# Plain float32 for the first block of a fused attention and feed-forward kernel

## The chip, the cores and the metric

The kernel runs on one core of a Trainium2 chip. The metric is the time of one execution on the device in microseconds; the median over several runs counts.

## The reference

A linear attention without softmax, a norm by head, and a feed-forward block with softplus. q, k, v have the shape 8 x 8 x 576 x 64 (batch, heads, sequence, head dimension), the two weight matrices are 512 x 2048 and 2048 x 512 and come in float64, as words of eight bytes.

```
kv  = einsum('bhsd,bhse->bhde', k, v)
out = einsum('bhsd,bhde->bhse', q, kv)
rms = sqrt(mean(out * out, axis=-1, keepdims=True) + 1e-06)
x   = (out / rms * g_norm).transpose(0, 2, 1, 3).reshape(4608, 512)
h   = x @ w_in
g   = maximum(h, 0) + log1p(exp(-abs(h)))
y   = g @ w_out                                  # 4608 x 512
```

## The kernel before

**Divided operands.** Large multiplications run in the format float32r, in which a multiplication rounds its operands. To keep float32 accuracy each operand is divided into a high part, a low part times 4096 and a third part that mends the product of both, and each product is three float32r multiplications into the same bank. Dividing an operand takes an operation on ScalarE (ACT) and two on VectorE (DVE): `high`, `low`, `less`. A weight's parts come from `split_weight`; for the eight weights of the first four chunks the third part is a sum made by two matmuls with the identity and its negative (`less_by_pe`, L525 and L526).

**Weights.** Weight number j belongs to chunk c = j // 2 of 128 hidden units; even j is a piece of w_in, odd j a piece of w_out. `weight` fetches it as two words for each value (512 KB) and makes a float32 of it: a square on ACT (L434), six operations on DVE (L438, L442, L447, L455, L460, L464), and an operation on ACT that counts values out of range (L451). There is one buffer `raw`, another `rawb`, and one `sq`. g of the norm is multiplied in when a piece of w_in is divided (L501, L508).

**Attention.** `kv_of(b)` loads k and v of a batch in four main parts and a tail and multiplies them (L696). `rows(t)` makes tile t of 128 tokens: q is turned (L776 on TensorE (PE) for the first two batches), multiplied by kv (L720), squared on ACT (L793), reduced on DVE (L724), its root taken on GpSimd (POOL, L727 and L728), scaled on DVE (L732), and turned (L738). The first six tiles are divided from the bank (`split`, L640, L643, L646) and stored to memory for later as well (L802, L803).

**Feed-forward.** The first stage walks over 12 blocks of 384 tokens, and in each over the first four or six chunks: `step(s)` is the multiplication by w_in (`mm1`, L864, 12 matmuls of 384 columns), softplus (L886), the division of g (L888, L875, L879) and the multiplication by w_out (`mm2`, L871, nine matmuls of 512 columns). Steps 0 to 3 are block 0, step 4 opens block 1. Two later phases do the other chunks in wide steps of 512 tokens with a scheme that saves multiplications (L1066, L1137), 48 of them.

**The order of the work.** Each operation is a task with an engine, an estimated duration, what it waits for, the buffers it takes and frees, and a position. `Plan.order` writes the order for every engine from these: an engine takes, of what can start first by the estimates, the task with the lowest position. The lists P0 to P7 are such positions. Where PE would stand idle by the estimates for 400 ns before step 6, a dummy matmul is put in (`warm`, L1232). The engines then run their lists strictly in order, and all DMAs of note are issued by SyncE (SP).

Of the kernel before, what the change touches and what calls it, by code (L numbers as in the profile page):

```python
# [22 lines left out]
DOWN_G = 1.0 - 0.99 * 2.0 ** -13  # L23
E = 1.0 / RADIX

# [181 lines left out]
def kernel(  # L207
# [47 lines left out]
    P0 = [-45.94, -26.77, -11.8, 0.28, -29.91, -5.64, -2.86, 3.84, -103.4, -98.98, -69.3, -76.66, -68.5, -24.67, -23.22, -34.97, 8.15, -43.02, 7.47, 9.69, 7.18, 18.16, -12.1, 4.75, 1.0, 106.19, 31.3, 6.28, 7.19, 5.22]  # L255
    P4 = [-30.17, -6.08, 16.93, -33.9, -22.35, -28.91, -17.33, -7.12, -18.68, -2.69, 0.62, 2.73, -7.38, -1.86, 1.1, 1.72, 5.22, -13.65, 3.22, 0.88, 43.88, 43.95, -0.17, -0.32, 44.8, 40.82, -20.17, -6.56, 6.41, 10.03, -10.73, 0.23, 2.8, 0.42, -9.48, -5.03]
    P5 = [1.24, -5.69, -2.28, -3.57, 1.72, 0.53, 6.68, -5.83, 3.01, -2.95, 3.35, 1.4, -6.96, 0.27, -5.34, -2.29]
    P6 = [1.05, 6.24, 4.29, 4.08, -1.52, -2.85, 1.21, -0.34, 3.11, 3.1, -1.07, -0.73, -0.88, 9.99, 5.7, 5.69, 0.13, 0.46]
    P7 = [-23.78, -17.98, -11.85, -14.93, 0.41, 1.61, 7.35, 2.7, -25.02, -6.6, -15.2, -4.48, -2.14, 0.64, 2.93, 0.97, 4.67, 5.36, 3.33, 6.57, -10.37, 2.36, -14.11, -9.89, -7.11, 12.91, -2.89, 14.55, 12.59, 9.35]
    CONVERT, FETCH, EARLY, LATER = P0[:8], P0[8:16], P0[16:27], P0[27:]  # L260
    P1 = [49.11, 48.77, 51.0, 80.9, 122.61, 131.29, 2.87, 53.84, 71.21, 480.08, 304.47, 150.69]
    P2 = [24.08, 35.56, 23.68, 37.26, 50.08, 83.13, 74.26, 112.0, 102.25, 108.09, 139.38, -110.13, 88.34, 208.35, 423.47, -209.77, 170.15, -245.78, 423.49, 179.94, -7.53]
    P3 = [2.14, 2.48, 6.41, -16.53, 0.86, 2.79, 4.01, -16.44, 3.79, 3.96, 2.19, 1.79, 0.72, 1.35, 1.55, -1.03]
# [3 lines left out]
    EARLIER = P3[15]  # L267
    PACE = 2.5
    BY_PE = 12
    AT_ONCE = 2 * TB  # L270

# [10 lines left out]
    g_down = const.tile([P, 1], F32, name="g_down")  # L282
# [24 lines left out]
    pieces = sb.tile([P, 12, PIECE], F32R, name="pieces")  # L307
    for i in range(3):
# [4 lines left out]
    minus_r = space("gv1", 4 * WIDE, False, F32R)[:, 3 * NT:3 * NT + P]  # L313
# [5 lines left out]
                 h=2, o=2, tp=1, s0=1, s1=1, s2=1, s3=1, w=15, wh=3, u=4, u1=1, gvp=2, xl=2, ab=2)  # L319
# [7 lines left out]
    heirs.update({("w", 12 + i): [("n", 3 * i + j) for j in range(3)] for i in range(3)})  # L327
    plan = Plan(rings, heirs)
    slot, add = plan.slot, plan.add

    def new(s, shape, dtype=F32):
# [17 lines left out]
        elif r == "w":  # L349
            s.tile = shaped(pieces[:, i] if i < 12 else space(f"w{i}", PIECE, True, F32R), shape, dtype)  # L350
        elif r == "n":
            s.tile = shaped(space(f"w{12 + i // 3}", PIECE, False)[:, i % 3 * d_model:], shape, dtype)
        elif r == "wh":
# [46 lines left out]
    factors_done = {}  # L400
# [13 lines left out]
    def weight(j, pos, fetch_pos, behind):  # L414

        c, of_out = divmod(j, 2)
        raw, w = slot("rawb" if j % 2 and c < 8 else "raw"), slot("m")
# [9 lines left out]
        if wide:  # L427
# [30 lines left out]
            def rest():  # L458
                pf = p.tile.bitcast(F32)
                nc.vector.scalar_tensor_tensor(out=pf, in0=words_of()[0], scalar=2.0 ** -52, in1=pf,  # L460
                                               op0=ALU.mult, op1=ALU.mult)

            def total():
                nc.vector.tensor_tensor(out=new(w, [P, d_model]), in0=t.tile.bitcast(F32),  # L464
                                        in1=p.tile.bitcast(F32), op=ALU.add)
# [6 lines left out]
            d4 = add("DVE", 430, power, [d3], pos, [p, w])  # L472
# [5 lines left out]
        if c < OWN:  # L478
            divide(j, w, ready, pos, c < 4)
# [11 lines left out]
    def split_weight(w, part_of, n, dst, ready, pos, of_in, by_pe=False):  # L491
# [21 lines left out]
        def low_up():  # L513
            nc.scalar.activation(dst.tile[:, 1], d.tile, func=AF.Copy, scale=RADIX)
# [753 lines left out]
```

## Time and profile before

| | |
|---|---|
| median of 3 runs | 857.7 us (857.61 to 859.12) |
| profiled execution, first to last instruction | 856.4 us |
| PE busy | 843.0 us, 98% |
| DVE busy | 704.1 us, 82% |
| ACT busy | 520.6 us, 61% |
| POOL busy | 76.6 us, 9% |
| moved by DMA | 167.07 MB, 195 GB/s over the span |

The span covers the instructions of the profiled execution; the difference to the median lies around them. Busy time of PE counts the dummy matmuls too, and ends of matmuls are modelled, so PE's share says little about the first microseconds.

### The profile page before, as it was taken

To read this page: it belongs to the slowest core of one execution; us is meant where nothing else is said; L and a number is where in the kernel's file an instruction comes from. 1 tells how busy PE (TensorE), PEld (TensorE's weight loads), DVE (VectorE), ACT (ScalarE), POOL (GpSimd) and SP (SyncE) were. 2 spreads that over 40 slices of the span, in tenths; PEclk is the share of its full clock that TensorE was granted. 3 is DMA by queue.
4 is the path that set the end of the run, shared out by engine and by line. 5 is a ranking of instruction groups with operands and counts; after the bars stand their busy time and mean duration, and the time that the engine had idled before them with its cause. 6 is when DMAs were issued, how large, how long until landed. Compare 5 with 4: busy or idle time off the path is not lost.

```text
span 856.4 us, 17075 instructions
## 1 busy us (share of the span) xinstructions
PE 843.0 (98%) x6464; PEld 754.1 (88%) x6464; DVE 704.1 (82%) x995; ACT 520.6 (61%) x980; POOL 76.6 (9%) x79
## 2 busy tenths in 40 slices
PE   8899999999999999999999999999999999999998
PEld 5578898999898999999999999998999899999996
DVE  7888898888788889798898788878788766788873
ACT  6766665446344567766667665655868555566654
POOL 0351223111113300000000000000000000000000
PEclk9999999999999999999999999999999999999999
DMA  9998997778884755436644546645364753777864
GB/s 283 297 233 212 261 273 232 185 245 218 214 188 119 194 160 185 142 110 207 210 156 154 180 151 206 195 158 181 124 197 138 234 168 102 240 237 246 249 189 131
DMA packets 239778, 167.07 MB, mean 195 GB/s; under 512 B 106320, under 2 KB 198736, under 8 KB 239696
## 3 DMA queue, kind: packets, MB, share of 16 engines
q1 hardware_dynamic: 239392, 165.86, 65.9%
q8 instruction: 50, 0.82, 0.4%
q14 instruction: 32, 0.26, 0.1%
q10 hardware_dynamic: 304, 0.13, 0.1%
HBM read 112.98 MB, written 52.95 MB: 194 GB/s over the span
## 4 chain that ended last, share of the span: by engine, by line
PE 94%; ACT 1%; DVE 1%; DMA 1%; issue 1%; POOL 0%; SPq 0%; POOLq 0%; DVEq 0%; ACTq 0%
PE banks L1137 31%; PE banks L1066 28%; PE banks L871 16%; PE banks L864 15%; PE banks L720 2%; PE banks L696 2%; DMA loads<-in_k_dram 1%; PE banks L738 0%; PE banks L1232 0%; PE banks L776 0%; DVE units L643 0%; DVE half L732 0%; DVE roots L724 0%; POOL roots L728 0%; ACT w L783 0%
## 5 line engine op out<-in xcount | busy, mean ns | idle before, releaser
L1137 PE MATMUL banks<-pieces,gv 128*128 128x512 f32 x768 | 236.8, 390 | 0.0
L1137 PE MATMUL banks<-pieces,g_False 128*128 128x512 f32 x384 | 149.4, 389 | 0.0
L1137 PEld LDWEIGHTS banks<-pieces,gv 128*128 128x128 f32 x768 | 132.5, 188 | 17.2 <-DVE banks L910 0.2
L864 PE MATMUL banks<-units,pieces 128*128 128x384 f32 x768 | 144.8, 337 | 0.0
L871 PE MATMUL banks<-pieces,gv 128*128 128x512 f32 x576 | 143.3, 393 | 0.0
L864 PEld LDWEIGHTS banks<-units,pieces 128*128 128x128 f32 x768 | 134.7, 188 | 4.5
L871 PEld LDWEIGHTS banks<-pieces,gv 128*128 128x128 f32 x576 | 106.2, 188 | 19.0
L1066 PEld LDWEIGHTS banks<-units,pieces 128*128 128x128 f32 x840 | 111.0, 188 | 6.5 <-ACT banks L1112 0.4
L1066 PE MATMUL banks<-units,pieces 128*128 128x256 f32 x840 | 115.2, 280 | 0.0
L886 ACT ACTIVATE half<-banks 128x384 f32<-128x384 f32 x64 | 31.4, 491 | 94.0 <-PE banks L864 90.7
L1127 DVE TENSOR_TENSOR gv<-g_True,gv 128x1024 fp32r<-128x1024 f32 x47 | 57.5, 1223 | 35.6 <-ACT gv L1124 35.5
L1137 PEld LDWEIGHTS banks<-pieces,g_False 128*128 128x128 f32 x384 | 72.1, 188 | 15.0
L1066 PEld LDWEIGHTS banks<-units,w 128*128 128x128 f32 x504 | 66.7, 188 | 3.7 <-ACT banks L1112 0.2
L1066 PE MATMUL banks<-units,w 128*128 128x256 f32 x504 | 69.6, 280 | 0.0
L728 POOL TENSOR_TENSOR roots<-roots,half 128x8 f32<-128x8 f32 x36 | 62.3, 1731 | 3.0
L1130 DVE SCALAR_TENSOR_TENSOR g_False<-gv 128x1024 fp32r<-128x1024 f32 x47 | 57.6, 1225 | 1.5
L1029 DVE TENSOR_TENSOR units<-loads,units 128x1024 fp32r<-128x1024 f32 x42 | 51.2, 1219 | 6.0 <-ACT units L1026 5.9
L1094 ACT ACTIVATE g_True<-banks 128x256 f32<-128x256 f32 x96 | 36.7, 384 | 30.6 <-PE banks L1066 29.9
L1116 DVE TENSOR_TENSOR g_True<-banks,g_True 128x512 f32<-128x512 f32 x48 | 33.1, 690 | 25.8 <-PE banks L1066 19.8
L931 ACT ACTIVATE m<-banks 128x512 f32<-128x512 f32 x72 | 42.1, 595 | 18.2 <-PE banks L1137 12.5
L1032 DVE SCALAR_TENSOR_TENSOR units<-units 128x1024 fp32r<-128x1024 f32 x42 | 51.4, 1224 | 1.7
L1026 ACT ACTIVATE units<-loads 128x1024 fp32r<-128x1024 f32 x42 | 44.3, 1056 | 12.4 <-PE banks L1066 10.1
(115 smaller groups left out, 1248.7 us busy)
## 6 DMA issues: line engine op xcount, KB each, us to landing
loads<-x SPq DMA_DIRECT2D x180, 128.0 KB, 2.7
part<-m SPq DMA_DIRECT2D x72, 256.0 KB, 3.1
m<-part SPq DMA_DIRECT2D x72, 256.0 KB, 3.4
loads<-form SPq DMA_DIRECT2D x45, 256.0 KB, 3.2
form<-loads SPq DMA_DIRECT2D x36, 256.0 KB, 3.0
raw<-in_moe_w_in_dram SPq DMA_DIRECT2D x16, 512.0 KB, 4.7
loads<-in_k_dram SPq DMA_DIRECT2D x32, 256.0 KB, 4.0
loads<-in_v_dram SPq DMA_DIRECT2D x32, 256.0 KB, 4.5
```

The lines of the kernel that those rows point to most:

```text
L728: nc.gpsimd.tensor_tensor(out=r.tile, in0=r.tile, in1=half, op=ALU.pow)
L864: nc.tensor.matmul(from_the_end(hp, w), lhsT=w_in.tile[:, i, kd * P:(kd + 1) * P], rhs=from_the_end(xv.tile[:, i, kd], w), start=(m == 0), ...
L871: nc.tensor.matmul(mine[i].tile, lhsT=gv.tile[:, m, i * P:(i + 1) * P], rhs=w_out.tile[:, m], start=(c == cs[0] and m == 0), stop=(c == cs ...
L931: a = add("ACT", 690 if ph == LAST else 600, lambda: nc.scalar.activation(new(ot, [P, d_model]), bank.tile, func=AF.Copy, scale=scale if p ...
L1026: nc.scalar.activation(part_of(0, F32R), xl.tile if m > 1 else xl.tile[:, 0], func=AF.Copy, scale=DOWN)
L1029: nc.vector.tensor_tensor(out=part_of(1, F32R), in0=xl.tile if m > 1 else xl.tile[:, 0], in1=part_of(0), op=ALU.subtract)
L1032: nc.vector.scalar_tensor_tensor(out=part_of(2, F32R), in0=part_of(1), scalar=-RADIX, in1=part_of(0), op0=ALU.mult, op1=ALU.add)
L1066: nc.tensor.matmul(from_the_end(place(q), (16, 8)[kd]), lhsT=w[:, m, at:at + P], rhs=from_the_end(dst.tile[:, m, v, kd] if u < 6 else dst. ...
L1094: nc.scalar.activation(dst, src, func=AF.Softplus, scale=1.0 + E)
L1127: nc.vector.tensor_tensor(out=gvt(1, F32R), in0=gt(), in1=gvt(0), op=ALU.subtract)
L1130: nc.vector.scalar_tensor_tensor(out=gt(F32R), in0=gvt(1), scalar=-RADIX, in1=gvt(0), op0=ALU.mult, op1=ALU.add)
L1137: nc.tensor.matmul(from_the_end(mine[i].tile, P), lhsT=(gvt(m, F32R) if m < 2 else gt(F32R))[:, c, i * P:(i + 1) * P], rhs=from_the_end(ou ...
```

## The change

Block 0 (`PLAIN = 1`) is multiplied in plain float32 with whole operands: `plain_step` does `mm1` with 4 matmuls of 384 columns and `mm2` with 3 of 512, and softplus goes straight into `mm2`. In steps 0 and 1 (`BY_TILES = 2`) `mm1` is done tile by tile, 12 matmuls of 128 columns, each tile as soon as it is there. x of block 0 is copied whole from the bank by ACT, and stored from that copy. The weights of chunks 0 to 3 are kept whole in a ring `f` of eight places; they are divided for block 1 at positions of their own (`DIVIDE`).

The pieces' buffers w1 to w11 hold other things while no piece needs them: two more buffers for raw weights (`rawc`, for chunks 1 and 3), four for the later parts of batch 0's k and v (`k0`), the eight whole weights, x of block 0 (`xf`).

g of the norm is multiplied in while a piece of w_in is made (`rest` and `total`). The division of a weight has two operations on ACT and two on DVE, with a scale that saves the third on ACT; the signs of `low` and `less` change with it, and the matmuls L525 and L526 fall away. All positions are new.

```diff
-    pieces = sb.tile([P, 12, PIECE], F32R, name="pieces")
+    pieces = sb.tile([P, 1, PIECE], F32R, name="pieces")
+    for i in range(1, 12):
+        space(f"w{i}", PIECE, False)
...
-        raw, w = slot("rawb" if j % 2 and c < 8 else "raw"), slot("m")
+        raw, w = slot("rawc" if c in (1, 3) else "rawb" if j % 2 and c < 8 else "raw"), slot("f" if c < 4 else "m")
...
+                    nc.vector.scalar_tensor_tensor(out=y, in0=tf, scalar=g_col, in1=pf, op0=ALU.mult, op1=ALU.add)
...
         if c < OWN:
-            divide(j, w, ready, pos, c < 4)
+            if c < 4:
+                plain[of_out, c] = w, [ready]
+                pos = DIVIDE[j]
+            divide(j, w, ready, pos, c < 4 and BANKED)
...
+            nc.scalar.activation(new(dst, [P, 3, n], F32R)[:, 0], src(), func=AF.Copy, scale=DOWN * E)
         def low():
+            nc.vector.scalar_tensor_tensor(out=dst.tile[:, 1], in0=dst.tile.bitcast(F32)[:, 0], scalar=RADIX, in1=src(),
+                                           op0=ALU.mult, op1=ALU.subtract)
-        def low_up():
-            nc.scalar.activation(dst.tile[:, 1], d.tile, func=AF.Copy, scale=RADIX)
+        def both_of():
+            f32 = dst.tile.bitcast(F32)
+            nc.vector.tensor_tensor(out=new(d, [P, n]), in0=f32[:, 0], in1=f32[:, 1], op=ALU.add)
...
-            ks, vs = (slot(f"tail{i}" if tail else "e") for i in range(2))
+            ks, vs = (slot(f"tail{i}" if tail else "k0" if not b and p > 1 else "e") for i in range(2))
...
+            def whole():
+                nc.scalar.copy(part_of_x(), x.tile)
+            def store():
+                nc.sync.dma_start(out=x_of(t), in_=part_of_x())
...
+    def plain_step(s, n, c, cs, h, g, xv, mine):
+        (w_in, in_done), (w_out, out_done) = plain[0, c], plain[1, c]
+        def mm1(i0=0, n=TB):
+            hp = (h.tile if i0 else new(h, [P, NT]))[:, i0 * P:(i0 + n) * P]
+            for kd in range(KD):
+                nc.tensor.matmul(hp, lhsT=w_in.tile[:, kd * P:(kd + 1) * P], rhs=xv.tile[:, kd, i0 * P:(i0 + n) * P],
+                                 start=(kd == 0), stop=(kd == KD - 1))
+        def mm2(i):
+            if c == cs[0]:
+                new(mine[i], [P, d_model])
+            nc.tensor.matmul(mine[i].tile, lhsT=g.tile[:, i * P:(i + 1) * P], rhs=w_out.tile,
+                             start=(c == cs[0]), stop=(c == cs[-1]))
...
+        if s < BY_TILES:
+            made = []
+            for i in range(TB):
+                made.append(add("PE", 910, lambda i=i: mm1(i, 1), [x_split[n][i]] + in_done + made[-1:], s + 0.1 * i,
+                                [] if i else [h], last, follows=None))
+            a = made[-1]
+        else:
+            a = add("PE", 2670, mm1, x_split[n] + in_done + [m for _, m in mm1s[-1:]] +
+                    (plain[1, ORDER[s - 2][1]][1] if s > 1 else []), s, [h], last)
...
+            a2 = add("PE", 880, lambda i=i: mm2(i), [a] + out_done + [mm2s.get(i)], s + AFTER,
+                     [mine[i]] if c == cs[0] else [], [g] + ([w_out] if n == PLAIN - 1 else []))
```

202 lines of the change are left out of this document (121 added, 81 removed).

## The prediction

> **What bounds the kernel now.** I read the page first, then the busy time by stage, then the instructions of TensorE by shape, then the timeline of the first 80 us.
>
> ```profile
> span 856.4 us, 17075 instructions
> PE 843.0 (98%) x6464; PEld 754.1 (88%) x6464; DVE 704.1 (82%) x995; ACT 520.6 (61%) x980; POOL 76.6 (9%) x79
> ```
> ```profile
> 0.00:44.09 44.09, 35.90 (x464) 25.97 (x465) 37.01 (x67) 31.51 (x61) 10.32 (x17) 1.00 1.01 285
> 44.09:78.84 34.75, 33.32 (x437) 27.55 (x436) 30.05 (x52) 22.32 (x45) 13.59 (x13) 1.00 0.89 226
> 78.84:357.38 278.54, 278.54 (x2417) 251.27 (x2416) 239.79 (x411) 154.94 (x305) 52.65 (x50) 1.00 0.73 200
> 357.38:852.60 495.22, 495.22 (x3153) 449.27 (x3151) 396.77 (x467) 311.39 (x570) 0.00 (x0) 1.00 0.58 182
> ```
> The columns of the second fence are the stage and its length, then busy time of PE, its weight loads, DVE, ACT, POOL, the granted clock, the DMA share and GB/s. From 78.84 us on PE is busy in every microsecond; a gain can only come from what lies before. There even the busy time flatters:
>
> ```profile
> L1232 PE MATMUL banks<-ident_r 128*128 128x512 f32 x52 | 18.8, 480 | 2.0 <-DVE ident_r L1192 1.6 <-ACT pieces L529 0.2
> L864 PE MATMUL banks<-units,pieces 128*128 128x384 f32 x60 | 11.7, 342 | 0.0
> L871 PE MATMUL banks<-pieces,gv 128*128 128x512 f32 x36 | 9.5, 399 | 0.0
> L696 PE MATMUL banks<-loads 128*64 128x64 f32 x224 | 8.9, 226 | 2.0 <-DMA loads<-in_v_dram 1.1 <-DMA loads<-in_k_dram 0.7 <-DVE units L643 0.2
> L720 PE MATMUL banks<-early,w 64*64 64x64 f32 x384 | 7.7, 223 | 1.2 <-ACT half L793 0.6 <-ACT w L802 0.4
> ```
> This is the window up to 78.84 us. L1232 is the dummy multiplication that fills gaps, 52 times. L864 stands 60 times: five first multiplications of twelve, so at 78.84 us step 5 begins. I compare the two kernels at that point, the start of step 5 (the second step of block 1), since PE is full from there on.
>
> **The price of plain float32.** Two rows of the chain give the dense rate of the divided steps:
>
> ```profile
> 123.58 4.20 PE banks L864 x24
> 127.78 4.08 PE banks L871 x18
> ```
> 4.20/24 = 0.175 us for 384 columns, 4.08/18 = 0.2267 us for 512: (0.2267 - 0.175)/128 = 0.404 ns a column, and 0.020 us fixed. A plain float32 multiplication that fills the array is not in the trace; L696 and L720 are plain float32 on parts of the array, 64 columns, with two records for each instruction of the program. Their record lasts 226 and 223 ns. The durations of L864 and L871 (342 and 399) rise by 0.445 ns a column from 171 ns, so 64 columns passed once would be 200 ns and passed twice 228 ns. So two passes for each of two records: four. A plain instruction then costs 4 x columns x 0.404 ns + 2 x 0.020 us: 0.867 us at 512, 0.660 at 384, 0.247 at 128. The new block 0 has 12, 8 and 24 of them: 10.4 + 5.3 + 5.9 = 21.6 us on PE. It drops 48 of L864 and 36 of L871: 8.4 + 8.2 = 16.6 us. PE gets 5.0 us more to do there; that all is bought for an earlier start.
>
> The Trainium skill, in "TensorE: Matmul & The Clock Gate", section Back-to-back issue gap, gives columns / 2.4 GHz + 2.5 ns for an isolated matmul: 162.5 ns at 384 and 215.8 at 512, less than the 175 and 226.7 that this trace has. By the page four passes each would come to an estimated 20.9 us, 0.7 us under my sum.
>
> **When the first multiplication can start.** Before, it waits for three divided tiles of x and the divided weights, at 44.09 us. In the changed program tile 0 alone does, against whole weights. What the list of its instructions shows ahead of that:
>
> ```profile
> 0.00:10.00 10.00, 7.48 (x39) 5.26 (x41) 6.57 (x16) 4.17 (x6) 1.06 (x7) 1.00 0.83 254
> 10.00:20.00 10.00, 8.52 (x93) 6.04 (x90) 8.84 (x16) 7.75 (x15) 0.00 (x0) 1.00 1.09 319
> raw<-in_moe_w_in_dram SPq DMA_DIRECT2D x16, 512.0 KB, 4.7
> loads<-in_k_dram SPq DMA_DIRECT2D x32, 256.0 KB, 4.0
> ```
> ```profile
> 4.73 0.43 DVE L438 TENSOR_SCALAR m<-raw 128x512 uint32<-128x512 uint32 x1 [1.68 <-DMA raw<-in_moe_w_in_dram]
> 18.62 0.69 PE L696 MATMUL banks<-loads 128*64 128x64 f32 x16 [0.72 <-DMA loads<-in_k_dram]
> 22.83 1.28 DVE L724 TENSOR_REDUCE roots<-half 128x8 f32<-128x512 f32 x2 [0.48 <-ACT half L793]
> 25.08 0.69 DVE L511 TENSOR_TENSOR m<-m,pieces 128x512 f32<-128x512 f32 x1
> 25.69 0.69 DVE L732 TENSOR_TENSOR half<-banks,roots 128x512 f32<-128x512 f32 x1
> 27.18 0.60 ACT L640 ACTIVATE units<-banks 128x512 fp32r<-128x512 f32 x1 [0.75 <-PE banks L738]
> ```
> DMA: before, the last main load of batch 0's k and v is the end of 4.98 MB in SP's list. With 2.54 MB by 10 us and 319 GB/s after, that is 17.65 us; its matmul starts at 18.62, so 1.0 us later. In the new list six weights stand ahead of that load instead of four, 6.29 MB in all: 10 + 3.75/0.319 + 1.0 = 22.8 us, 4.2 us later than before. From that matmul to the first reduce of a tile are 22.83 - 18.62 = 4.2 us: 27.0 us.
>
> DVE: a weight's conversion is L438, L442, L447, L455, L460 and L464, 0.42 + 0.69 + 0.69 + 0.42 + 0.69 + 0.69 = 3.6 us by these groups of the whole run:
>
> ```profile
> L438 DVE TENSOR_SCALAR m<-raw 128x512 uint32<-128x512 uint32 x24 | 10.0, 415 | 2.0 <-DMA raw<-in_moe_w_in_dram 1.9
> L442 DVE SCALAR_TENSOR_TENSOR m<-raw,m 128x512 uint32<-128x512 uint32 x24 | 16.6, 690 | 0.6
> L455 DVE TENSOR_SCALAR m<-m 128x512 uint32<-128x512 uint32 x32 | 13.6, 424 | 1.2 <-DMA part<-m 0.4
> L464 DVE TENSOR_TENSOR m<-m,m 128x512 f32<-128x512 f32 x32 | 22.0, 687 | 0.7
> L451 ACT ACTIVATE sq<-sq,big 128x512 bf16<-128x512 bf16 x32 | 23.0, 717 | 8.1 <-DVE m L447 7.8
> L451 ACT ACTIVATION_READ_ACCUMULATOR sq<-sq,big 128x1 f32 x32 | 6.1, 190 | 0.0
> ```
> (the two not shown have L442's shape). Ahead of the first reduce the new DVE list has three whole conversions, a fourth but for its last operation, two operations each of three more, and four operations of dividing: 10.8 + 2.9 + 3.3 + 2.8 = 19.8 us. From 4.73 us on, with 2.1 us idle until the third weight (3.93 MB, 15.4 us) lands, that is 26.6. DMA and DVE meet at 27.0.
>
> From the reduce to the tile in SBUF took 27.18 + 0.60 - 22.83 = 4.95 us, which gives 31.95. But ACT now has ahead of that copy the count of what lies out of range (0.72 us and its 0.19 read) for a weight whose mask is the eighth operation of DVE from the reduce on; that is done at 31.9, the count at 32.9, the copy at 33.5. So the first useful multiplication starts at 33.5 us, 10.6 us earlier. It is not 10.6 us of gain, as PE has by then done less: the new list has three groups of k and v and several turns and rows still to come.
>
> **From there to step 5.** PE's list between: 21.6 us of plain float32, one L864 step (2.1 us), 3.5 turns of q, 7 of x, 8 of rows, 8 groups of k and v. Their start-to-start times:
>
> ```profile
> 39.48 0.66 PE L776 MATMUL banks<-ident_r,w 128*128 128x128 f32 x4
> 40.07 0.69 PE L720 MATMUL banks<-early,w 64*64 64x64 f32 x32
> ...
> 51.86 1.15 PE L696 MATMUL banks<-loads 128*64 128x64 f32 x32 [0.21 <-DVE units L643]
> 52.95 0.69 PE L720 MATMUL banks<-early,w 64*64 64x64 f32 x32
> 53.57 2.38 PE L864 MATMUL banks<-units,pieces 128*128 128x384 f32 x12
> ...
> 78.43 0.66 PE L738 MATMUL banks<-ident_r,half 128*128 128x128 f32 x4
> 78.84 2.36 PE L864 MATMUL banks<-units,pieces 128*128 128x384 f32 x12
> ```
> A turn of q 0.59, two groups of k and v 1.09, rows 0.62, a turn of x 0.41: 2.1 + 4.4 + 5.0 + 2.9. With the 23.7 above it is 38.0 us. I add 1.0 us for tile 2, whose copy comes eight ACT operations behind its norm. Step 5 at 33.5 + 38.0 + 1.0 = 72.5 us, if nothing else waits.
>
> What can wait is W_out of chunk 1: its total stands last in DVE's list, 40 operations after the first reduce, and the second multiplication of step 1 needs it. PE reaches that one at 33.5 + 19.1 + 1.0 = 53.6. The 40 are 35 of 0.69 and 5 of 0.42. Independent neighbours start 0.61 us apart (L511 to L732 above), dependent ones 0.72: with 0.65, 22.8 + 2.1, and 0.4 allowed for a norm that waits for its root on POOL (2.86 us from reduce to norm above), so the total ends at 27.0 + 25.3 + 0.7 = 53.0, just in time. By full durations, 26.3 us, at the share of 10 to 20 us (8.84 of 10): 29.7, the end at 57.4, and PE stands 3.8 us: step 5 at 76.3. I take 74.0, nearer the lower end, as that sum has the waits for DMA, POOL and ACT in it already.
>
> At its step 5 the old kernel has, by the order of both lists, done two groups of k and v, one of rows and one turn of x more: 1.09 + 0.62 + 0.41 = 2.1 us. So 76.7 is what 74.0 stands against: 2.7 us gained.
>
> **Edits with no cost of their own.** Dividing without the third ACT operation frees ACT, which is no bound (61%). The weights of block 0 are divided on DVE and no more with 16 matmuls; that is eight operations of 0.69 us, and DVE drops six of that size and eight of 384 columns, the division of x and g in block 0, so it has less in all. The cover is plain float32 on PE; without it these 5.5 us would lie ahead of step 4. g moves into operations that exist. The stores of x in block 0 wait for ACT's copy in SP's list; ahead of the first of them SP has issued 10.5 MB, which at the rates above last to 35 us, past the copy at 33.5, so the queues do not run dry. Positions anew: from step 5 on I count nothing, since both lists hold the same matmuls and PE has no idle time to win.
>
> **The rivals.** (a) DVE at its early pace: step 5 at 76.3, 0.4 us gained, 857.3. For it: DVE is busy 37.01 of the first 44.09 us and still late. Against it: the conversions have their weights loaded earlier. (b) Slower: the first reduce stands in DVE's in-order list with all conversions behind it, so late k and v hold back everything. If six weights come at the 254 GB/s of the first 10 us, the load lands at 24.8 + 1.0, 3.0 us later; with (a) step 5 is at 79.3, 2.6 us lost, 860.3. It decides from a first reduce after 29 us at DVE's early pace, or 31 us at mine. (c) Slower: new positions open waits in the wide steps.
>
> ```profile
> 414.35 2.80 PE banks L1066 x24
> ```
> A wide step is 42 x 0.1167 + 24 x 0.2267 = 10.34 us, 48 of them 496; the stage above took 495.2, so nothing can be won and 0.1 us lost in each would be 4.8 us: 859.8, after the gain. (d) A plain instruction takes half the passes: 10.8 us less, of which DVE's total at 53.0 lets some 7 through: 848. The record durations speak against it.
>
> **How the numbers follow.** The span is 856.4 and the median 857.7; the 1.3 us around the span I leave as they are. 857.7 - 2.7 = 855.0. In (c) 4.8 is 2.1 more than the gain. Chances: my forecast 0.52, (a) 0.19, (b) 0.19, (c) 0.06, (d) 0.04. A measurement of this kernel tells 0.2%, 1.7 us, from no change. Faster 0.56, same 0.19, slower 0.25. Low end: no idle DVE ahead of the third weight and no count ahead of the copy, 2.1 and 1.5 us off 72.5 with half a microsecond lost again: about 69.4 to 70, 851.0. High end: (b), 860.3, set at 860.5. Left out are (d) and the tails.
>
> **What would show it.** Right: the first plain multiplication at 32 to 36 us, a plain 512 column instruction near 0.87 us, step 5 at 73 to 75, PE full after. Wrong: a first reduce after 29 us; PE waiting for the total of W_out before step 1's second multiplication for over 3 us; idle PE after 80 us.

## The result: 1.8% slower

The changed kernel takes 873.4 us (median of 4 runs, 872.02 to 875.12), the kernel before 858.3 (4 runs, 857.61 to 859.12): ratio 1.0176, 95% interval 1.0161 to 1.0192. The forecast was 855.0 us, with a range of 851.0 to 860.5. The profiled execution took 873.92 us with a span of 872.1, 15.7 us over the span before. One execution of e5 below, 939.58 us at a granted clock of 0.85, is left out as a slow one; all other times are of fast executions. The head of the page of the changed kernel, and the busy time by stage (columns as in the prediction; the stages begin at the first plain multiplication, at step 5 and at the first wide step, with a mark at 140 us between):

```profile
span 872.1 us, 16972 instructions
PE 853.5 (98%) x6455; PEld 753.6 (86%) x6455; DVE 703.5 (81%) x988; ACT 491.1 (56%) x928; POOL 77.4 (9%) x79
```
```profile
0.00:37.91 37.91, 28.89 (x296) 21.52 (x296) 28.24 (x52) 18.17 (x36) 4.89 (x11) 0.95 0.90 266
37.91:80.54 42.63, 39.30 (x530) 27.47 (x528) 35.83 (x58) 28.41 (x57) 16.49 (x14) 1.00 0.88 230
80.54:140.00 59.46, 57.23 (x620) 49.80 (x616) 50.58 (x88) 32.08 (x62) 18.21 (x18) 1.00 0.88 228
140.00:337.72 197.72, 197.59 (x1733) 178.06 (x1729) 167.63 (x289) 96.88 (x192) 37.79 (x36) 1.00 0.72 197
337.72:868.28 530.56, 530.55 (x3295) 476.76 (x3294) 420.73 (x503) 315.05 (x582) 0.00 (x0) 1.00 0.57 177
```

Step 5 begins at 80.54 us. Against 76.7 for the kernel before, at equal work done, that is 3.8 us lost, where 2.7 were to be gained. From there to 140 us PE is idle for 2.2 us, where before it was never idle. The last row shows PE busy in every microsecond, and still the stage is longer. The busy share doesn't show the loss; the number of multiplications in equal time (in brackets behind PE's busy time) does. Two stretches of the wide stage, before and then after:

```profile
400.00:600.00 200.00, 200.00 (x1274) 181.58 (x1273) 169.83 (x207) 121.61 (x229) 0.00 (x0) 1.00 0.56 175
600.00:800.00 200.00, 200.00 (x1276) 181.53 (x1275) 156.32 (x175) 130.64 (x236) 0.00 (x0) 1.00 0.60 191
```
```profile
400.00:600.00 200.00, 200.00 (x1256) 179.84 (x1255) 164.29 (x201) 116.84 (x222) 0.00 (x0) 1.00 0.55 174
600.00:800.00 200.00, 200.00 (x1261) 179.77 (x1260) 158.02 (x178) 119.53 (x216) 0.00 (x0) 1.00 0.58 181
```

In the same 400 us the rows count 2517 multiplications instead of 2550, 1.3% fewer. The timeline of PE shows where: in stretches of twelve and more multiplications of 256 columns, after and then before.

```profile
507.11 1.61 PE L1153 MATMUL banks<-early,w 128*128 128x256 f32 x12
508.56 2.35 PE L1153 MATMUL banks<-units,w 128*128 128x256 f32 x18
510.74 0.88 PE L1153 MATMUL banks<-units,pieces 128*128 128x256 f32 x6
511.46 0.63 PE L1224 MATMUL banks<-w,gv 128*128 128x512 f32 x2
```
```profile
500.35 0.86 PE L1066 MATMUL banks<-early,pieces 128*128 128x256 f32 x6
501.05 0.86 PE L1066 MATMUL banks<-turned,half 128*128 128x256 f32 x6
501.75 1.56 PE L1066 MATMUL banks<-units,w 128*128 128x256 f32 x12
503.15 0.62 PE L1137 MATMUL banks<-pieces,gv 128*128 128x512 f32 x2
```

After, 36 take 511.46 - 507.11 = 4.35 us, 121 ns each; before, 24 take 2.80 us, 117 ns each. The waits of PE's weight loads from 400 us on (who waited, for whom, us in total, times, longest) show what stands ahead of such stretches, after and before:

```profile
PEld banks L1153 <- ACT banks L1199: 5.3, 24, 0.2
```
```profile
PEld banks L1066 <- ACT banks L1112: 0.6, 3, 0.2
```

L1199 is ScalarE's copy of a bank in a wide step (L1112 before). The new positions let PE come to the product that needs the copy while the copy is still being made.

To compare the stages of all runs I gave each multiplication the median distance to the next one of its shape in the kernel before (117 ns for 256 columns, 227 for 512; plain float32 by its own median) and none to a dummy; what is left of the time is lost. Lost up to 80, 140 and 340 us and to the end, in us:

| kernel | 80 | 140 | 340 | end |
|---|---|---|---|---|
| before | 31.1 | 32.4 | 34.7 | 34.5 |
| after | 35.4 | 40.0 | 42.9 | 50.7 |
| after, old wide positions (e1) | 34.9 | 39.6 | 42.5 | 44.5 |
| before, new wide positions (e2) | 30.2 | 31.8 | 33.9 | 49.1 |
| after, kept busy (e11) | 34.4 | 39.0 | 41.9 | 49.5 |
| after, old P3 alone (e12) | 33.5 | 38.2 | 41.1 | 55.8 |
| after, all mended (e14) | 33.6 | 37.0 | 39.6 | 41.7 |

TensorE's work by this count is 817.7 us before and 817.2 after: the change is neutral there. All of the loss is waiting or a slower pace: 4.3 us by 80 us, 3.9 up to 340 us, 8.0 in the wide stage.

The first of these shares is uncertain. The lists of all engines are the same in the changed kernel, e1, e7 and e12 up to 298 us, as only positions of the wide stage differ. Yet step 5 begins at 80.54 us in the first, at 80.15 in e1, and in e7 and e12 here:

```profile
78.93 2.35 PE L915 MATMUL banks<-units,w 128*128 128x384 f32 x12
```
```profile
78.67 2.35 PE L915 MATMUL banks<-units,w 128*128 128x384 f32 x12
```

So one execution tells the time of step 5 to some 2 us only, and smaller differences between runs ahead of 80 us are not clear of that. Between 80 and 340 us the changed kernel, e1, e11 and e12 lose 7.5, 7.6, 7.5 and 7.6 us, which agree.

### The profile page after: what moved, and what is told of

The parts are those of the page before. It is cut to its first block, busy times and chain, and to the rows that moved or that the text cites. A ratio compares the mean times of both kernels' runs of the same rounds, so it can differ in the third digit from the quotient of the medians.

```text
span 872.1 us, 16972 instructions
## 1 busy us (share of the span) xinstructions
PE 853.5 (98%) x6455; PEld 753.6 (86%) x6455; DVE 703.5 (81%) x988; ACT 491.1 (56%) x928; POOL 77.4 (9%) x79
## 4 chain that ended last, share of the span: by engine, by line
PE 93%; DMA 2%; DVE 2%; ACT 1%; POOL 1%; SPq 1%; issue 1%; DVEq 0%; ACTq 0%
PE banks L1224 30%; PE banks L1153 28%; PE banks L915 14%; PE banks L922 14%; PE banks L766 2%; PE banks L742 2%; PE banks L960 1%; DMA g<-in_moe_w_out_dram 1%; DVE half L778 1%; POOL roots L774 1%; PE banks L966 1%; DMA loads<-in_k_dram 1%; DMA g_col<-in_g_norm_dram 1%; PE banks L784 1%; SPq L812 0%
## 5 line engine op out<-in xcount | busy, mean ns | idle before, releaser
L1224 PE MATMUL banks<-w,gv 128*128 128x512 f32 x768 | 238.7, 392 | 0.0
L1224 PE MATMUL banks<-w,g_False 128*128 128x512 f32 x384 | 149.3, 389 | 0.0
L1224 PEld LDWEIGHTS banks<-w,gv 128*128 128x128 f32 x768 | 132.3, 188 | 17.4
L1153 PEld LDWEIGHTS banks<-units,w 128*128 128x128 f32 x996 | 132.0, 188 | 8.5 <-ACT banks L1199 1.1
L1153 PE MATMUL banks<-units,w 128*128 128x256 f32 x996 | 137.4, 282 | 0.0
L922 PE MATMUL banks<-w,gv 128*128 128x512 f32 x540 | 135.8, 394 | 0.0
L922 PEld LDWEIGHTS banks<-w,gv 128*128 128x128 f32 x540 | 99.1, 188 | 17.6 <-DVE gv L930 0.3
L915 PE MATMUL banks<-units,w 128*128 128x384 f32 x588 | 110.8, 336 | 0.0
L915 PEld LDWEIGHTS banks<-units,w 128*128 128x128 f32 x588 | 103.3, 188 | 3.7
L1224 PEld LDWEIGHTS banks<-w,g_False 128*128 128x128 f32 x384 | 72.1, 188 | 15.9
L1214 DVE TENSOR_TENSOR gv<-gv,g_True 128x1024 fp32r<-128x1024 f32 x47 | 57.5, 1223 | 30.8 <-ACT gv L1211 30.5
L1153 PE MATMUL banks<-early,w 128*128 128x256 f32 x516 | 71.6, 286 | 0.0
L1153 PEld LDWEIGHTS banks<-early,w 128*128 128x128 f32 x516 | 65.9, 188 | 5.5 <-ACT banks L1199 4.3
L1017 ACT ACTIVATE m<-banks 128x512 f32<-128x512 f32 x72 | 41.8, 594 | 15.4 <-PE banks L922 8.4
```

The lines of the kernel that those rows point to most:

```text
L915: nc.tensor.matmul(from_the_end(hp, w), lhsT=w_in.tile[:, i, kd * P:(kd + 1) * P], rhs=from_the_end(xv.tile[:, i, kd], w), start=(m == 0), ...
L922: nc.tensor.matmul(mine[i].tile, lhsT=gv.tile[:, m, i * P:(i + 1) * P], rhs=w_out.tile[:, m], start=(c == cs[0] and m == 0), stop=(c == cs ...
L1017: a = add("ACT", 690 if ph == LAST else 600, lambda: nc.scalar.activation(new(ot, [P, d_model]), bank.tile, func=AF.Copy, scale=scale if p ...
L1153: nc.tensor.matmul(from_the_end(place(q), (16, 8)[kd]), lhsT=w[:, m, at:at + P], rhs=from_the_end(dst.tile[:, m, v, kd] if u < 6 else dst. ...
L1214: nc.vector.tensor_tensor(out=gvt(1, F32R), in0=gvt(0), in1=gt(), op=ALU.subtract)
L1224: nc.tensor.matmul(from_the_end(mine[i].tile, P), lhsT=(gvt(m, F32R) if m < 2 else gt(F32R))[:, c, i * P:(i + 1) * P], rhs=from_the_end(ou ...
```

## The experiments

Fifteen kernels were run, each against the kernel before on the same chip. Theory A puts the wide loss on the new positions; the rivals for the start are that k and v come late (B, E), that too few loads are under way (D), that the halved clock costs (K), that plain float32 itself sets the pace (L), or that VectorE's list does (C, F). Theory M is on the order of TensorE's list behind step 5, P on positions that fit one set of durations only.

**e1 and e2: the wide positions.** P3, shown here, and the eighteen values of P6 are exchanged; e2 is the mirror.

```
-    P3 = [-8.02, 0.12, 7.72, -0.99, 3.54, 3.59, 3.64, -0.4, 3.59, 3.59, -0.55, 1.9, -16.47, -73.53, -77.35, 7.71]
+    P3 = [2.14, 2.48, 6.41, -16.53, 0.86, 2.79, 4.01, -16.44, 3.79, 3.96, 2.19, 1.79, 0.72, 1.35, 1.55, -1.03]
```

> The changed kernel with the old positions of the wide stage alone (P3 and P6; the lists of the engines are the same up to the entry into the wide steps). Theory A (the new positions of the wide stage cost time: its six-matmul pieces start right behind an eviction, PE's weight loads wait for ScalarE's bank, and the matmuls after such a wait come 120 ns apart instead of 117): the 8.0 us that TensorE loses after 340 us go, 865.4 us (864.4 to 866.4), and the wait of the weight loads of the first product for the bank falls from 5.3 us to under 1. Rival (the loss lies in the operations themselves, as the new split and scale, or in the state that the block stage leaves): 872 to 874 us, the wait stays.

> The mirror: the kernel before with the new P3 and P6 alone. Theory A: 8.0 us more, 866.3 us (865 to 867.5), and the weight loads of the first product wait some 5 us for the bank. Rival (the positions only hurt together with the new operations): 858 to 860 us.

e1: 867.24 us, ratio 1.0104 (1.0089 to 1.0119). Its rows of the wide stage and of the wait:

```profile
400.00:600.00 200.00, 200.00 (x1275) 181.40 (x1274) 162.77 (x195) 117.73 (x222) 0.00 (x0) 1.00 0.54 173
600.00:800.00 200.00, 200.00 (x1271) 181.21 (x1270) 158.60 (x184) 122.21 (x220) 0.00 (x0) 1.00 0.60 186
```
```profile
PEld banks L1153 <- ACT banks L1199: 1.0, 4, 0.3
```

The old density is back: 2546 multiplications in the 400 us. 6.2 us are gained of the 8.0 expected; 2.0 are still lost after 340 us, most of it at the entry into the wide steps. e2: 873.81 us (1.0164 to 1.0196): the kernel before loses 15.4 us, twice what was expected, all of it after 340 us. So the positions carry the wide loss, in both kernels, and how much depends on the lists they meet.

**e12: P3 alone.** The edit of e1 with the new P6 kept.

> The changed kernel with the sixteen old positions of a wide step (P3), the new ones of the units (P6) kept. If P3 alone holds the loss of the wide stage: 867 us (866 to 868.3), the weight loads of the first product wait under 1.5 us for the copied bank. If the positions of the units' loads (P6) matter as much: 869.5 to 872 us.

879.81 us (1.0228 to 1.0259), slower than either set.

```profile
400.00:600.00 200.00, 199.21 (x1249) 177.81 (x1249) 158.59 (x190) 115.50 (x216) 0.00 (x0) 1.00 0.53 170
```

Neither expectation holds. P3 and P6 are a set: 14.7 us lost after 340 us with half of it exchanged.

**e7: two positions of P3.** LATE sets when products 4 to 6 of a wide step come.

```
-    P3 = [..., 1.9, -16.47, -73.53, -77.35, 7.71]
+    P3 = [..., 1.9, 0.72, 1.35, -77.35, 7.71]
```

> The changed kernel, with two of the sixteen wide positions as before: those of products 4 to 6 of a wide step (LATE: 0.72 and 1.35 instead of -16.47 and -73.53), which in the changed kernel come as soon as ScalarE has copied a bank for them. Theory A in its narrow form (that copy is what the weight loads wait for, 24 times 0.2 us, and what leaves half of the first products 121 ns apart): the waits for the copy fall under 1.5 us, the pieces at over 119 ns from 915 of 2016 to under 300, and TensorE's loss after 400 us from 7.6 to 2 to 3 us: 868.5 us (867.5 to 870). Rival (it is the positions of the second product, or all of them together): the waits go elsewhere, 871 to 876 us.

874.88 us (1.0168 to 1.0201): no gain. The waits for the copy fall from 24 to 16, and multiplications of 256 columns at 119 to 125 ns from 893 to 622, but other waits of up to 1.3 us take their place, and by the count of the table the loss behind 340 us is about 2.5 us larger than in the changed kernel. The narrow form of theory A fell; which values matter is open.

**e3: a buffer for the last v.** The ring of four new buffers gives one up early, and the last load goes to the third again.

```
-            ks, vs = (slot(f"tail{i}" if tail else "k0" if not b and p > 1 else "e") for i in range(2))
+            ks, vs = (slot(f"tail{i}" if tail else "e" if b or p < 2 else "k1" if p == 3 and i else "k0") for i in range(2))
-    ... k0=4)
+    ... k0=3, k1=1)
```

> The changed kernel, but the last load of v of batch 0 gets the fourth of the four new buffers, which the ring leaves unused (its load goes to the third once more and waits for that one's multiplication). All lists stay the same. Theory B (the start is bound by when k and v of batch 0 are there): the load is issued 2 us earlier, its multiplication starts at 23 instead of 25.2 us, the first reduce at 27.4 instead of 29.5, step 5 at 78.6 instead of 80.5, 871.4 us (870.6 to 872.2). Rival C (VectorE's list of conversions is the bound, whose first idle time is the 3.9 us before the third weight): the multiplication moves as much, the reduce by under 1 us, and the time by under 0.7: 872.7 to 873.8.

872.83 us (1.0153 to 1.0183), 0.6 less, too little to tell from none. The load was issued at 17.70 us instead of 20.21, but it took 7.7 us to land instead of 4.9, and the multiplication stayed at 25.5 us (25.24 in the changed kernel). Neither expectation holds: the moment of issue did not set when this load landed.

**e4: other loads first.** With e3's buffer; the tasks of the planner's list are moved by index.

```
+    for t in loads_of[8:12]:
+        todo.remove(t)
+    at = todo.index(loads_of[6])
+    todo[at:at] = loads_of[8:12]
...
-        nc.scalar.dma_start(out=g_col[e * D:(e + 1) * D], in_=g_norm.rearrange("(d one) -> d one", one=1))
+        nc.gpsimd.dma_start(out=g_col[e * D:(e + 1) * D], in_=g_norm.rearrange("(d one) -> d one", one=1))
```

> The same, and also: the two loads each of the second and third tile of q go behind two loads of k, one of v and W_out of chunk 0; and g of the norm is loaded from GpSimd's queue. Theory D (at most eight DMAs are under way: each waits for the eighth before it; in the changed kernel the ninth waits 2.1 us for the tiny load of g, and then six small loads of q keep only 1 MB under way): the wait for g goes, the first 10 us move over 245 GB/s instead of 215, W_out of chunk 0 lands at 14 instead of 18.3 us, VectorE's idle 3.9 us there falls under 0.5, the first reduce starts at 26 (25 to 27), step 5 at 77 (76 to 78.5), 869.9 us (868.5 to 871.4). Rival (the rate of the DMA engines, not their number under way, is the bound): under 230 GB/s in the first 10 us, W_out after 16.5 us, no gain over the run with its own buffer alone.

874.61 us (1.0167 to 1.0201). The weight (it is W_out of chunk 2, not 0) did land by 14.8 us, but the queues behind it now waited for q: PE's turn first, then ScalarE's copies, and VectorE for ScalarE's square, which stands behind those:

```profile
15.25 1.08 PE L824 MATMUL banks<-ident_r,early 128*128 128x128 f32 x4 [3.12 <-DMA early<-in_q_dram]
19.34 0.69 DVE L467 SCALAR_TENSOR_TENSOR m<-sq,m 128x512 f32<-128x512 bf16 x1 [3.36 <-ACT sq L454]
```

The first 10 us moved 225 GB/s, not over 245, and the next ten 319: 0.3 MB more by 20 us than the changed kernel. The edit also had a cost of its own: with the load of g on GpSimd, VectorE waited 1.38 us at 8 us for a value that GpSimd makes from g. Theory D's wait was there, but taking it away gained nothing; that it costs nothing in a better list is not shown.

**e8: half of the plain first product.** The other half of that sum is left out.

```
-            for kd in range(KD):
+            for kd in range(KD // 2):
```

> The changed kernel, but the first product of block 0 sums only the first half of its inner dimension: its 32 plain multiplications become 16, so 5.3 us less work on TensorE between 38 and 66 us, in the same order (it leaves out half of that sum). Theory L (TensorE's own work sets the pace there, so plain float32 is paid in full): 5.0 us less, 868.4 us (867.4 to 869.5). Rival F (VectorE's conversions and norms set the pace up to step 4, and plain float32 is hidden): under 2 us less, 871.4 to 873.4 us, TensorE idle instead.

870.62 us (1.0122 to 1.0168): 2.8 us less for 5.3 us of work. By the medians about half of that plain float32 is paid, the rest was waiting, so neither L nor F holds alone. The share is rough: the runs of e8 lie 3.7 us apart, and its step 5 at 78.00 us is 0.7 us ahead of that of e12, which has all the work.

**e5, e6 and e9: k and v ahead of two weights.** They stand on e1 with e3's buffer, which was not run by itself; I estimate it at 867.2 - 0.6 = 866.6 us. `behind(engine, which, at)` moves the tasks of these indices behind another; e6 adds dummies to e5, e9 takes fourteen away from it instead, and lets ScalarE copy q first.

```
...
+    behind("SP", (15, 17), 18)
+    behind("DVE", (26, 27), 35)
+    behind("DVE", (30, 31), 40)
+    behind("DVE", (23, 24), 42)
...
+    for i in range(36, 50):
+        todo.remove(of["PE"][i])
+    behind("ACT", (20, 21), 22)
```

> The changed kernel with the old wide positions and the own buffer of the last load of v (the two runs before: 867.2, and 0.6 less for the buffer, so 866.6 us is what this stands against), and with two of the six weights that are loaded ahead of the last k and v (W_in of chunks 2 and 3) behind them, and the six conversion operations that VectorE does for them and one more weight ahead of the first reduce behind it. Nothing is left out. Theory E (the order of loads and conversions holds the first plain multiplication back, and what follows goes with it): last v multiplied at 22 instead of 25.5 us, first reduce at 26.3 instead of 29.5, first plain multiplication at 34.8 instead of 37.9, step 5 at 78 instead of 80.5, 864.0 us (863 to 865.2). Rival F (the conversions that now come later are needed soon after, VectorE's list as a whole sets the pace up to step 4): the first reduce moves by 3 us, step 5 by under 0.8, 866 to 867 us.

> The run before it, and eleven more of the dummy multiplications where TensorE stands idle: four ahead of the first of k, one and three ahead of v's, one ahead of the first rows, two ahead of the first turn of x. Theory K (an idle TensorE of 2 us at 8 to 10 us has the clock granted at half for 3.4 us some 3 us later, and that slows the turns and products of the start): the granted clock stays 1.00 in every stretch up to 60 us, and 0.5 to 1.5 us are gained on the run before. Rival (the start waits for loads and VectorE, so half a clock costs nothing there, and the dummies stand in the way): within 0.5 us of the run before, or slower.

> The run with the two later weights (867 to 868.7 us, step 5 as before) once more, but without fourteen of the fifteen dummy multiplications that stood ahead of the last k and v in TensorE's list: there they ran until 25.6 us and hid that the load was there. And ScalarE copies the first turned tile of q ahead of a count that waits for VectorE. Theory E: last v multiplied at 22 us, first reduce at 26 (25.3 to 27) instead of 29.4, first plain multiplication at 33 to 35 instead of 37.9, step 5 at 78 instead of 80.5, 864.3 us (863 to 865.5) against 866.6. Rival F (VectorE's list as a whole sets the pace up to step 4): the first plain multiplication moves by 3 us or more, step 5 by under 0.8, 866 to 867.5 us, and TensorE waits between 50 and 75 us instead.

e5: 867.7 us (867.09 to 869.63), ratio 1.0109 (1.0087 to 1.0131). e6: 868.17 (1.0088 to 1.0125). e9: 868.71 (1.0095 to 1.0128). None gains. In e5's list the dummies still stood ahead of the last v, and in e6, which adds three there, its multiplication came at 25.60. In e9 it came at 22.21, and then:

```profile
27.39 1.28 DVE L772 TENSOR_REDUCE roots<-half 128x8 f32<-128x512 f32 x2 [1.05 <-ACT half L841]
39.63 2.70 PE L962 MATMUL banks<-w,w 128*128 128x128 f32 x16
81.34 2.35 PE L917 MATMUL banks<-units,w 128*128 128x384 f32 x12
```

The reduce moved by 2.1 us, but the first plain multiplication came 1.7 us later and took 2.70 us instead of 1.95, and step 5 came at 81.34: from 35 to 41 us the clock was granted at about half (0.59, 0.50, 0.50 and 0.70 in the stretches from 34 to 42 us). The same work, from a group of rows to the end of that product, took 6.70 us from 35.56 us on, against 4.20 from 35.59 on in the changed kernel, without a wait in either: 2.5 us at half the clock. Theory E fell as stated, and the run does not tell the order of loads from the clock.

**e11: the changed kernel, kept busy.** 25 more dummies and nothing else.

```
...
+    for i, n in ((13, 8), (26, 1), (33, 3), (49, 5), (53, 2), (64, 3), (68, 3)):
+        at = todo.index(of["PE"][i]) + 1
+        todo[at:at] = [spare] * n
```

> The changed kernel and nothing but more dummy multiplications (25) in TensorE's waits of the first 36 us: eight more ahead of the first k, one and three more ahead of two of v's, five ahead of the last v, two ahead of the rows, three ahead of a turn of q, three behind the first turn of x. Theory K (each stretch of some 2 us in which TensorE stands idle is followed by 3.4 us at half the granted clock, which comes in some runs twice or three times, and costs about 1 us each): the granted clock is 1.00 in every stretch of 2 us up to 60, all runs lie within 0.7 us of each other, and the median is 871.7 us (871.2 to 872.2), where the changed kernel's one run at a mean clock of 1.0 lay, against 873.4. Rival (half a clock costs nothing where TensorE waits for others): 873 to 874.5 us, at whatever clock.

872.44 us (872.01 to 873.82; ratio 1.0146 to 1.0177). The stretches from 8 to 16 us, of the changed kernel and then of e11 (the number before the last two is the granted clock):

```profile
8.00:10.00 2.00, 0.12 (x4) 0.15 (x6) 1.93 (x4) 1.05 (x4) 0.00 (x0) 1.00 1.18 328
10.00:12.00 2.00, 2.00 (x22) 1.91 (x22) 1.97 (x4) 0.37 (x2) 0.00 (x0) 0.71 1.08 238
12.00:14.00 2.00, 2.00 (x8) 1.27 (x7) 1.89 (x4) 1.32 (x3) 0.00 (x0) 0.50 0.96 299
14.00:16.00 2.00, 1.94 (x10) 1.07 (x8) 0.45 (x1) 1.60 (x4) 0.00 (x0) 0.94 0.86 292
```
```profile
10.00:12.00 2.00, 1.80 (x19) 1.23 (x15) 1.93 (x4) 1.01 (x2) 0.00 (x0) 1.00 1.17 249
12.00:14.00 2.00, 1.63 (x11) 1.19 (x11) 1.93 (x4) 1.81 (x4) 0.00 (x0) 1.00 0.97 306
```

The clock stays at 1.00 and the median is 1.0 us lower, less than the 1.7 expected; one run was still at 873.82, and the intervals of the two ratios overlap. Nor does the halved clock go with a late start: in e7 it was granted at 0.68, 0.50, 0.50 and 0.61 in the stretches from 8 to 16 us, and step 5 came at 78.93 us, against 79.51 in e11. Theory K is not shown for this place, where much of PE's time goes to dummies. It has a price where PE has work and does not wait, as at 35 us in e9.

**e10 and e14: the block stage, and all together.** e10 is e9 with three moves in PE's list. One of them runs the first product of step 12 ahead of VectorE's last operation on a tile that it reads, so that a wait it needs is missing; e14 does without that move, and takes e1, e3 and e11's dummies with it. The two moves of e14:

```
...
+    behind("PE", (128,), 129)
+    behind("PE", (170,), 167)
```

> The run before it, and three moves in TensorE's list between 84 and 126 us: a turn of x one piece of the second product later, and the first products of steps 12 and 13 ahead of rows that wait for a bank. Theory M (TensorE's idle time after 80 us, 0.77, 0.62 and 0.85 us in the changed kernel, comes from rows and turns that the new positions put too close behind one another, not from VectorE's load): those three waits go, 1.5 to 2.2 us less than the run before. Rival (VectorE and ScalarE are behind there as a whole): the waits turn up at the next rows, under 0.6 us less.

> The old positions of the wide stage (P3 and P6), the own buffer of the last v, the dummies of the run that keeps TensorE busy, and two moves in TensorE's list: a turn of x at 87 us one piece of the second product later, and the first product of step 13 right behind that of step 12, ahead of rows that wait for their bank. Expected as a sum: 873.4 - 6.2 (wide) - 0.6 (buffer) - 1.7 (clock) - 1.5 (the waits at 87 and 125 us) = 863.4 us (862.3 to 865). If the shares overlap (the clock's and the buffer's both lie in TensorE's waits of the start): 865 to 867 us. Either way it stays over the kernel before, by the start and the block stage.

e10: 867.43 us (1.0088 to 1.0123), 1.3 less than e9 with overlapping intervals, and part of it may be the missing wait. e14: 864.57 us (1.0052 to 1.0101), within 1.2 us of the sum of the shares. Between 80 and 140 us it loses 3.4 us instead of the 4.6 of the changed kernel (the kernel before: 1.3), and of the three waits there of 0.77, 0.62 and 0.85 us only that of 0.62 is left: theory M holds for the two that were moved. It is the fastest version with the change, and 5.8 us over the kernel before.

**e13: the new division at the old positions.** PLAIN = 0, the old buffers and all old positions: what is left of the change is g in the conversion and two ScalarE operations instead of three, with their signs and scales.

> The kernel before, its positions and buffers, with the new division alone (g of the norm in the conversion of the weights, two operations on ScalarE for a divided weight instead of three, the difference by TensorE for the first eight as before, signs and scales with it); the lists are made anew from the old positions, as the durations are others. Theory P (the division costs nothing by itself, and positions fit one set of durations only): TensorE's busy first products and the clock as before, but new waits from the lists: 862 to 885 us, the loss again after 340 us for the most part. Rival Q (positions carry over to a slightly other kernel): 857 to 860 us.

883.73 us (1.0265 to 1.0322). The lists made anew from the old positions lose more than all of the change does. Its wide stage is nearly as dense as before; the loss lies ahead of it, which theory P did not say, with 4.7 us idle at the entry:

```profile
343.69:400.00 56.31, 51.58 (x300) 47.38 (x299) 44.95 (x66) 34.61 (x66) 0.00 (x0) 0.97 0.45 139
```

**e15: k and v first, kept busy.** e14 with e9's order of loads, one norm ahead of a total, and the dummies set anew for it.

```
...
+    behind("DVE", (42,), 39)
...
+    for i in range(44, 50):
+        todo.remove(of["PE"][i])
```

> The last run (864.6 us; first reduce 29.17, first plain multiplication 37.51, step 5 at 78.77) with the order of loads and conversions of the late weights put on top: W_in of chunks 2 and 3 loaded behind the last k and v, six conversion operations behind the first reduce, the second norm ahead of one total, and dummies that keep TensorE busy in the waits this order leaves, so that the clock stays at 1.00. Theory E (k and v of batch 0 hold the start back, and where the order of the weights was mended before, the halved clock ate it): last v multiplied at 22.5, first reduce at 26.5 (26 to 27.5), first plain multiplication at 35.7 (35 to 36.3), step 5 at 77.2, 863.0 us (862.2 to 863.9). Rival F (VectorE has to do the same conversions before the second product of step 1 anyway and sets step 5): the first plain multiplication 1.5 us earlier, step 5 within 0.5 us of 78.8, 864 to 865.3 us.

867.12 us (1.0069 to 1.0107), 2.5 more than e14.

```profile
26.94 1.28 DVE L772 TENSOR_REDUCE roots<-half 128x8 f32<-128x512 f32 x2 [1.08 <-ACT half L841]
38.58 0.69 PE L744 MATMUL banks<-loads 128*64 128x64 f32 x16 [2.20 <-DMA loads<-in_v_dram]
39.76 3.51 PE L962 MATMUL banks<-w,w 128*128 128x128 f32 x16
```

The reduce is where theory E had it (26.94). But ahead of the first plain multiplication PE's list has two groups of k and v of batch 1, whose loads now come behind the weights, and it waited for them, 1.34 and 2.20 us. Behind the second wait the clock was at half in spite of the dummies (0.50 from 40 to 42 us), the first plain product took 3.51 us, and step 5 came at 82.29. Mending one load makes the next one late. What the start would be with the whole list of loads made for it stays open.

## Why the prediction was wrong, step by step

The miss is 18.4 us: 6.5 by step 5 (80.54 against 74.0, of which up to 1.9 is the spread of the start), 11.9 behind it. The rows of the changed kernel's timeline that answer to the steps:

```profile
18.36 0.43 DVE L456 TENSOR_SCALAR m<-g 128x512 uint32<-128x512 uint32 x1 [3.90 <-DMA g<-in_moe_w_out_dram]
25.24 0.69 PE L742 MATMUL banks<-w,w 128*64 128x64 f32 x16 [1.45 <-DMA w<-in_v_dram]
29.47 1.28 DVE L770 TENSOR_REDUCE roots<-half 128x8 f32<-128x512 f32 x2
35.35 0.57 ACT L673 COPY w<-banks 128x512 f32<-128x512 f32 x1
37.91 1.95 PE L960 MATMUL banks<-w,w 128*128 128x128 f32 x16
53.35 1.88 PE L966 MATMUL banks<-w,half 128*128 128x512 f32 x4
55.07 2.74 PE L960 MATMUL banks<-w,w 128*128 128x384 f32 x8
57.74 0.69 PE L766 MATMUL banks<-early,w 64*64 64x64 f32 x32
59.18 0.68 DVE L484 TENSOR_TENSOR w<-m,m 128x512 f32<-128x512 f32 x1
80.54 2.35 PE L915 MATMUL banks<-units,w 128*128 128x384 f32 x12
```

**The price of plain float32 was right.** Two records make an instruction: 57.74 - 55.07 = 2.67 us for four of 384 columns, 0.667 each (forecast 0.660), and 55.07 - 53.35 = 1.72 for two of 512, 0.86 each (0.867). Rival (d) is out.

**When k and v are there: 22.8 forecast, 25.24 measured.** The step that failed is the rates of the old kernel for the new list. The first 20 us, one issue row and one wait of SP's queue:

```profile
0.00:10.00 10.00, 6.28 (x18) 4.61 (x20) 5.65 (x14) 3.67 (x6) 0.94 (x7) 1.00 0.71 215
10.00:20.00 10.00, 8.73 (x75) 6.39 (x74) 5.81 (x10) 4.49 (x9) 0.00 (x0) 0.83 1.00 299
```
```profile
3.32 6.96 SPq L812 DMA_DIRECT2D early<-in_q_dram  x6
```
```profile
SPq L812 <- DMA g_col<-in_g_norm_dram: 2.1, 1, 2.1
```

215 and 299 GB/s instead of 254 and 319: 0.6 MB less by 20 us, about 1.9 us. SP spent 7 us on six loads of q with 128 KB each. In this program a load waits for the eighth before it, so the second of q waited for the tiny load of g. That this wait and the small loads made the rate low is in part argued: in e4, without the wait and with larger loads ahead, half of the 0.6 MB came back by 20 us, and k and v were there no earlier. That the third weight landed at 18.3 us made VectorE idle for 3.9 us, where I had allowed 2.1.

**First reduce: 27.0 forecast, 29.47 measured**, just past the 29 us that I had set as the sign of rival (b). **First plain multiplication: 33.5 forecast, 37.91 measured.** 2.5 of it is the reduce; ScalarE's copy ended at 35.92 (forecast 33.5), as late as the reduce and no later. I had taken the copy's end for the multiplication's start; PE's list has rows, a turn of q, a group of k and v and a turn of x between, 2.0 us. From there to step 5 I had 40.5 us (74.0 - 33.5), 2.5 of them for waits; it took 42.6, with PE idle for 3.3.

**The total of W_out of chunk 1: 53.0 forecast, 57.4 by the slower sum, 59.9 measured** (59.18 + 0.68). PE got to it at 59.95 with no wait to speak of, so the sign that I had named (PE waiting there for over 3 us) did not show: both were 6 to 7 us late. Step 5 at 80.54 us is 1.2 us later than the 79.3 of rival (b). As far as the start goes it was that rival's size. Its mechanism as I told it, late k and v alone, is not shown: bringing them forward gave nothing in e9 and e15.

**"From step 5 on I count nothing": the step that failed most.** I argued that PE had no idle time to win and both lists held the same work, and so left out what could be lost. It lost 11.9 us there: 3.9 up to 340 us, 8.0 in the wide stage. The waits up to 140 us:

```profile
88.93 0.66 PE L784 MATMUL banks<-ident_r,half 128*128 128x128 f32 x4 [0.77 <-ACT w L850]
119.87 0.69 PE L766 MATMUL banks<-early,w 64*64 64x64 f32 x32 [0.62 <-ACT half L839]
125.90 1.16 PE L766 MATMUL banks<-early,w 64*64 64x64 f32 x64 [0.85 <-DVE half L778]
```

Rows and turns stand too close behind one another there: moving two of them took two of these waits away in e14. What else makes up the 3.9 us is not shown. Rival (c) had the waits of the wide stage, though not the slower pace behind them, and nearly the size (4.8 us forecast, 6.2 to 8.0 measured), but a chance of 0.06, and it was set against the gain, not added to the loss of (b). (b) and (c) together are 860.3 + 4.8 = 865.1; nothing in the range had both. The positions of 48 equal steps were the part of the change with the largest lever, and I gave them one sentence.

**Edits at no cost.** The division costs nothing on PE (817.7 and 817.2 us of work), but e13 shows that its other durations are not free: the planner makes other lists of them, and with positions that were not made for these 25 us are lost.

## What to carry to other kernels

Where a list is made from positions, a change of a duration or a position can change every stage. Price it at the steps that repeat most, as waits times repeats, and let rivals add up. Before a difference between two traces is explained, look how far apart the same list comes out in two executions. When PE is busy throughout, count multiplications per microsecond in equal stretches; the busy share hides a loss of 1.3%. In a start that is full of loads, one load brought forward shows the next late one: look down the lists of all engines for what waits next, before a gain is promised.

## What the runs showed of the hardware

An idle TensorE of 2.1 us (7.75 to 9.88) was followed by half the granted clock: 0.71, 0.50 and 0.94 in three stretches of 2 us are 1.16 + 2.0 + 0.24 = 3.4 us at half. It came in some executions of a kernel and not in others: the four of the changed kernel had mean clocks of 1.0, 0.996, 0.997 and 0.994 with spans of 870.2, 871.1, 872.1 and 873.3 us. In e8 TensorE was idle for 3.29 us at the same place (6.60 to 9.88), and the clock stayed at 1.00: the length of the idle time alone does not decide it. The Trainium skill, in "TensorE: Matmul & The Clock Gate", section What's actually happening, has a free-running window of about 3.4 us, after an idle one of which the clock is halved. The length and the half agree; that 2.1 us of idle time were enough does not.

After a weight load that waited some 0.2 us for a bank, the next multiplication came 150 to 210 ns behind the one before it, and multiplications of 256 columns then ran on at 119 to 125 ns instead of 117, up to 29 in a row: 893 of the 1834 in the wide stage from 400 us on, against 17 of 1794 in the kernel before. That pace adds up to some 3.2 us, the 45 longer distances to 2.6 us, and slower multiplications of 512 columns to some 2 us: about the 8.0 us that the wide stage loses. What keeps up the slower pace is not shown.
